# Attention scores of a chunk from three products on two halves of the array, instead of four products on the whole of it

## The chip, the core and the metric

The program runs on one core of a Trainium2 chip. The metric is the device time of one execution in microseconds (us), as the median over runs; the profile comes from one further execution.

## What is computed

Three stages follow one another: an attention with a threshold (4 batches, 8 heads, 576 positions, 64 values per head), a squared-ReLU feed-forward layer on its result (512 to 2048 to 512), and a mixture of 8 experts in which each token goes to one. The change touches only the scores of the attention:

```python
scores = scale * np.matmul(q, k.transpose(0, 1, 3, 2))
thresh = np.max(scores, axis=-1, keepdims=True) - tau
scores = np.where(scores >= thresh, scores, -1000000000.0)
attn = softmax(scores)          # written out in the reference
out = np.matmul(attn, v)
h = np.maximum(x @ w_in, 0.0); g = h * h; x = g @ w_out
# then: gate, one of 8 experts per token, two more products
```

## The kernel before

Products are taken in float32r, a rounded form of float32. To keep precision, an operand is split in a rounded part ("hi") and the rest ("lo", again rounded); a product of two operands is then a sum of terms hi·hi, hi·lo, lo·hi and, where wanted, lo·lo.

The attention runs over 16 pairs of heads (`pr`); a pair has 9 chunks of up to 128 queries (`STEPS`): four of head 0, four of head 1, and one (`hd == 2`) with the last 64 queries of both heads in one block-diagonal operand `xd`. That makes 144 chunks, numbered `n`. A chunk's work passes through all engines: scores on TensorE (`mm`, L636) against all 576 keys, in two halves of 288 in two banks of PSUM; maximum on VectorE (L639); exponential on ScalarE (L642); threshold and sum on VectorE (L651); division on GpSimd or ScalarE (L662, L695); five 128x128 transposes on TensorE (L705); copies out of PSUM on ScalarE (L713). Twice in a pair `t_av` (L733) multiplies with the values: ten products in two column halves of the array, 64 columns for each head, alternating between them. From the second batch on, the first feed-forward product (`t_h`, L843; 12 matmuls per unit, cut in three groups of four) of the batch before is interleaved with the chunks of the next batch.

The operands of a pair lie with head 0 on partitions 0-63 and head 1 on 64-127: `xk` and `xq` (index 0 hi, 1 lo). Three forms of the score product stand side by side in `t_chunk`:

- Chunks 0 to 3 (`n < EARLY`, L672) multiply directly on the head's 64 partitions, four terms for two halves: 8 matmuls of 64 rows. Chunks 0 and 1 are of head 0 (rows 0-63), chunks 2 and 3 of head 1 (rows 64-127).
- The block-diagonal chunk (`hd == 2`) uses 128 rows, three terms, 6 matmuls.
- All others (124 of the 144) use `opA` or `opB`, built for each head by `t_op`: for the keys, hi on partitions 0-63 and lo on 64-127; for the queries, the two parts in one order and in the other. Two passes of 128 rows, each for two halves, hold all four terms: 4 matmuls of 128 rows. To build them `t_op` issues five copies from SBUF to SBUF for each head on SyncE's queue (two `put_k`, one `put_q`, two `turn_q`), ten for a pair.

The order of all work is written out ahead by a list scheduler (`Graph.schedule`): each task has an engine, an assumed duration (`c_pe` and the like), a due time (`key`) and its reads and writes; engines then run their instructions in that fixed order. Buffers come from pools with a fixed number of slots; a buffer is given back after its last reader.

Of the kernel before, what the change touches and what calls it, by code (L numbers as in the profile page):

```python
# [9 lines left out]
F32 = mybir.dt.float32  # L10
# [201 lines left out]
def c_act(n, psum=False, ptr=0):  # L212
    return n / 1200 + (0.051 if psum else 0.093) + 0.093 * ptr


def c_dve(n, rate=1):
    return n / 960 / rate + 0.068


def c_pe(n):  # L220

    return n * 0.4227e-3 + 0.0123


def c_dma(nbytes):
    return 2.0 + nbytes / 150e3
# [35 lines left out]
def moa(ctx, tc, q, k, v, tau, w_in, w_out, wg, wog, w1, w2, ctab, coln, out):  # L262
    nc = tc.nc
    B, H, S, D = 4, 8, 576, 64
    P = 128
# [7 lines left out]
    HALF = S // 2  # L273
# [20 lines left out]
    OPN = S + 2 * 512  # L294
# [31 lines left out]
    g = Graph()  # L326
# [17 lines left out]
    def K(nm, pr):  # L344
        return PLACE[nm][pr >= NP]
# [88 lines left out]
        at = mk(nm, at, n, shape)  # L434
    at = 0
    for nm, n, shape in (
        ("xk", 2, [P, 2, S]), ("xq", 1, [P, 2, S]), ("xd", 1, [P, 2, P]),
        ("opA", 2, [P, OPN]), ("opB", 2, [P, OPN]),
    ):
        at = mk(nm, at, n, shape, F32R)  # L440
    ATT = 128 + 4 * NFC * P + 2 * 2 * NKC * 256 + 2 * (DFE // P) * 256
# [71 lines left out]
    def new(nm, tag):  # L513
        return Buf(ALL[nm], f"{nm}{tag}")

    def dma(fn, nbytes, r, w, key, q="SP", rel=0.0):
        dur = max(0.66, nbytes / 340e3)
        g.add(q, dur, fn, r, w, key, lat=c_dma(nbytes) - dur, rel=rel)

    raws, xks, xqs, xds, opb, xTb, wb = {}, {}, {}, {}, {}, {}, {}  # L520
# [27 lines left out]
    def q_tags(pr, x):  # L548
        return [(xqs[pr], x)] if pr else [(xqs[pr], x, i) for i in range(2)]
# [30 lines left out]
        g.add("ACT", c_act(S, False, nm == "q"), hi, [raw], [(xy, 0)], key - 1)  # L580
        g.add("DVE", 0.87, lo, [raw, (xy, 0)], [(xy, 1)], key - 1)

    def t_op(pr, j, key):

        xk, xq = xks[pr], xqs[pr]
        buf = opb[pr, j] = new("opB" if j else "opA", f"{pr}")
        rows = slice(64 * j, 64 * j + 64)
        q3 = lambda r: buf.t[r, S:].rearrange("p (x n) -> p x n", x=2).bitcast(F32)

        def put_k(x):  # L590
            nc.sync.dma_start(buf.t[64 * x : 64 * x + 64, :S].bitcast(F32), xk.t[rows, x].bitcast(F32))

        def put_q():
            nc.sync.dma_start(q3(slice(0, 64)), xq.t[rows, :, 64:].bitcast(F32))

        def turn_q(x):
            nc.sync.dma_start(q3(slice(64, 128))[:, 1 - x], xq.t[rows, x, 64:].bitcast(F32))

        parts = lambda xy, *xs: [t for x in xs for t in (q_tags(pr, x) if xy is xq else [(xy, x)])]
        for x in range(2):  # L600
            dma(lambda x=x: put_k(x), 64 * S * 4, parts(xk, x), [(buf, "k", x)], key)
        dma(put_q, 64 * 1024 * 4, parts(xq, 0, 1), [(buf, "q")], key)
        for x in range(2):
            dma(lambda x=x: turn_q(x), 64 * 512 * 4, parts(xq, x), [(buf, "t", x)], key)

    def t_diag(pr, key):

# [7 lines left out]
    def t_chunk(n, key):  # L615
        pr, st = divmod(n, NST)
        hd, c = STEPS[st]
        s = Buf(pS if n >= SWAP else pS0, f"s{n}")
        p = new("p", n)
        nm, th, sm = (new(x, n) for x in ("nm", "th", "sm"))  # L620
        heads = (0, 1) if hd == 2 else (hd,)
        halves = [slice(hf * HALF, (hf + 1) * HALF) for hf in range(2)]
        q0 = QOFF[c]
        xk = xks[pr]

        def mm():
            if hd == 2:

                xd = xds[pr].t
                ops = [(xd[:, x], xk.t[:, y]) for x, y in ((0, 0), (0, 1), (1, 0))]  # L630
            else:
                o = opb[pr, hd].t
                ops = [(o[:, S + i * 512 + q0 : S + i * 512 + q0 + P], o[:, :S]) for i in range(2)]
            for i, (qo, ko) in enumerate(ops):
                for hf in range(2):
                    nc.tensor.matmul(s.t[:, hf, :HALF], qo, ko[:, halves[hf]], start=(i == 0), stop=(i == len(ops) - 1))  # L636

        def mx():
            nc.vector.tensor_reduce(nm.t, s.t[:, :, :HALF], axis=AX.XY, op=ALU.max, negate=True)  # L639

        def ex():
            nc.scalar.activation(  # L642
                p.t[:, :S].rearrange("p (a n) -> p a n", a=2), s.t[:, :, :HALF], AF.Exp, bias=nm.t
            )

        def thr():
            nc.gpsimd.tensor_scalar(th.t, nm.t, -1.0, ntau, op0=ALU.mult, op1=ALU.add)  # L647

        def msk():
            p3 = p.t[:, :S].rearrange("p (a n) -> p a n", a=2)  # L650
            nc.vector.scalar_tensor_tensor(  # L651
                p3, s.t[:, :, :HALF], th.t, p3, op0=ALU.is_ge, op1=ALU.mult, accum_out=sm.t
            )

        def r1():
            nc.gpsimd.tensor_scalar(sm.t, sm.t, 1.0, 1e-9, op0=ALU.mult, op1=ALU.add)

        def r2():
            nc.vector.reciprocal(sm.t, sm.t)  # L659

        def nrm():
            nc.gpsimd.tensor_scalar(p.t[:, :S], p.t[:, :S], sm.t, 1.0, op0=ALU.mult, op1=ALU.mult)  # L662

        if n < EARLY:
            xq = xqs[pr]
            hr = slice(64 * hd, 64 * hd + 64)

            def mm():
                i = 0
                for qx, kx in ((0, 0), (0, 1), (1, 0), (1, 1)):  # L670
                    for hf in range(2):
                        nc.tensor.matmul(  # L672
                            s.t[:, hf, :HALF], xq.t[hr, qx, 64 + q0 : 64 + q0 + P], xk.t[hr, kx, halves[hf]],
                            start=(i == 0), stop=(i == 3),
                        )
                    i += 1

            rd = [(xk, x) for x in range(2)] + [(xq, x, 0) for x in range(2)]
            g.add("PE", c_pe(HALF) * 8, mm, rd, [s], key)
        elif hd == 2:  # L680
            rd = [(xk, x) for x in range(2)] + [(xds[pr], j) for j in range(2)]
            g.add("PE", c_pe(HALF) * 6, mm, rd, [s], key + K("scores", pr))
        else:
            o = opb[pr, hd]
            rd = [(o, "q")] + [(o, w, x) for w in "kt" for x in range(2)]
            g.add("PE", c_pe(HALF) * 4, mm, rd, [s], key + K("scores", pr))
        g.add("DVE", c_dve(S), mx, [s], [nm], key + K("max", pr))
        g.add("ACT", c_act(S, True, 1), ex, [s, nm], [p], key + K("exp", pr))
        g.add("POOL", 0.36, thr, [nm], [th], key + K("bound", pr))
        g.add("DVE", c_dve(S) + 0.085, msk, [s, th], [p, sm], key + K("mask", pr))  # L690
        g.add("POOL", 0.22, r1, [], [sm], key + K("sum", pr))
        g.add("DVE", 0.09, r2, [], [sm], key + K("sum", pr))
        if pr < NP and hd == 0 and c % 2:
            g.add("ACT", c_act(S, False, 1),
                  lambda: nc.scalar.activation(p.t[:, :S], p.t[:, :S], AF.Copy, scale=sm.t), [sm], [p],  # L695
                  key + K("norm", pr))
        else:
            g.add("POOL", 0.85, nrm, [sm], [p], key + K("norm", pr))

        for x, (a, z) in enumerate(TCUT):  # L700
            ps = Buf(pT[x], f"pT{n}_{x}")

            def tr(ps=ps, a=a, z=z):
                for i in range(a, z):
                    nc.tensor.transpose(ps.t[:, i - a], p.t[:, i * P : (i + 1) * P], ident)  # L705

            g.add("PE", 0.109 * (z - a), tr, [p], [ps], key + K("turn", pr))
            for j, gi, c0, w, off in PARTS[st]:
                if (pr, gi) not in ptb:
                    ptb[pr, gi] = new("pt", f"{pr}_{gi}")  # L710
                pt = ptb[pr, gi]
                g.add("ACT", c_act((z - a) * w, True),
                      lambda pt=pt, ps=ps, j=j, a=a, z=z, c0=c0, w=w, off=off: nc.scalar.activation(  # L713
                          pt.t[:, j, a:z, off : off + w], ps.t[:, :, c0 : c0 + w], AF.Copy),
                      [ps], [(pt, j, off, x)], key + K("parts", pr))
# [240 lines left out]
    rows = {}  # L956
# [412 lines left out]
    def pair_prep(pr, key):  # L1369
        for nm in "kqv":  # L1370
            t_load(pr, nm, key - 8)
        for nm in "kq":
            t_qk(pr, nm, key)
        for j in range(2):
            t_op(pr, j, key)
        t_diag(pr, key)

    pair_prep(0, -100)
    t_fill(5)
    wkey = {i: (W0 + 2.25 * i) * T0 for i in range(NFC)}  # L1380

    for pr in range(NPR):
# [3 lines left out]
        for st in range(NST):  # L1386
            n = pr * NST + st
# [54 lines left out]
    for i in range(22):  # L1442
        n = 160 if i < 8 else 256
# [12 lines left out]
    with tc.If(more > 0):  # L1456
        for tab, lo, hi, U in ((tab2, S2, NL2, 2), (tab1, S1, NL1, 1)):
            n = nc.values_load(tabn[0:1, 2 - U : 3 - U], min_val=0, max_val=hi)
# [49 lines left out]
```

## Time and profile before

| | us |
|---|---|
| time, median of 3 runs | 967.85 |
| lowest and highest of them | 965.61 and 968.86 |
| the profiled execution's own time | 965.47 |
| its span in the trace | 963.7 |
| TensorE busy in it | 932.3 (97%) |
| VectorE / ScalarE / GpSimd busy | 716.4 / 645.6 / 361.3 |

TensorE is busy nearly throughout. The trace models the ends of matmuls, and they overlap in the engine's pipeline: a row's duration is not what a matmul costs in a row of others. What it costs is the distance from one start to the next. A row of the timeline merges neighbouring instructions of one line; with n of them, the distance is the row's length less the duration of the last one, divided by n - 1. A window of 10 ns shows the instructions in flight at that moment, and the start of the oldest.

### The profile page before, as it was taken

Reading aid. Unit: us, or ns where it says so; the run is one execution under the profiler, and the core shown is the slowest. Engines: PE = TensorE matmul, PEld = TensorE weight load, DVE = VectorE, ACT = ScalarE, POOL = GpSimd, SP = SyncE. Lnnn points to the kernel's source line nnn. Section 1 sums busy time; section 2 is a strip of 40 time slices with the busy share of each in tenths; the row PEclk is TensorE's granted clock in tenths of the full one; section 3 lists DMA queues with packets and bytes.
Section 4 is the critical chain, followed back from the end, with each engine's and each line's share of the span. In section 5 each row is a group of like instructions: output and inputs, shape, how many; then the busy total and the mean of one; then the engine's idle time right before and its main releaser. Section 6 shows DMA issues by size and latency. Waiting matters only on the chain. (4 is left out here: it accounts for less than half of the span.)

```text
span 963.7 us, 20604 instructions
## 1 busy us (share of the span) xinstructions
PE 932.3 (97%) x6842; PEld 846.0 (88%) x6842; DVE 716.4 (74%) x1635; ACT 645.6 (67%) x1431; POOL 361.3 (37%) x607
## 2 busy tenths in 40 slices
PE   7899999999999999999999999999898999999996
PEld 6667889889889889989999999999887989889895
DVE  6898988877777777788558767898778677777720
ACT  5898888878678777787554444444648676876731
POOL 4556778875656766642101000010113111211300
PEclk9999999999999999999999999999999999999999
DMA  6785797767778766478455888566959867977700
GB/s 176 181 221 141 204 253 201 213 166 212 234 214 231 228 198 201 158 226 246 136 143 133 190 185 194 134 171 140 260 170 338 307 229 262 309 248 257 264 23 25
DMA packets 162565, 193.25 MB, mean 201 GB/s; under 512 B 23567, under 2 KB 113167, under 8 KB 162450
## 3 DMA queue, kind: packets, MB, share of 16 engines
q1 hardware_dynamic: 158210, 181.33, 65.2%
q0 software_dynamic: 4096, 10.52, 3.5%
q8 instruction: 56, 0.92, 0.4%
q14 instruction: 59, 0.48, 0.2%
q10 hardware_dynamic: 144, 0.00, 0.0%
HBM read 122.39 MB, written 43.20 MB: 172 GB/s over the span
## 5 line engine op out<-in xcount | busy, mean ns | idle before, releaser
L651 DVE SCALAR_TENSOR_TENSOR memf<-banks,memf 128x576 f32<-128x576 f32 x144 | 116.3, 814 | 43.4 <-ACT memf L642 27.0
L843 PE MATMUL banks<-memr,w 128*128 128x288 f32 x960 | 145.0, 299 | 1.3 <-DVE memr L740 1.3
L843 PEld LDWEIGHTS banks<-memr,w 128*128 128x128 f32 x960 | 130.9, 188 | 5.3 <-issue 3.8
L1004 PE MATMUL banks<-w,memr 128*128 128x256 f32 x864 | 126.9, 284 | 0.0
L713 ACT ACTIVATE pt<-banks 128x384 f32<-128x384 f32 (+2 forms) x320 | 114.2, 419 | 14.0 <-PE banks L705 13.5
L642 ACT ACTIVATE memf<-banks,memf 128x576 f32<-128x576 f32 x144 | 107.1, 753 | 20.1 <-DVE memf L639 13.6
L984 ACT ACTIVATE memr<-memf 128x512 fp32r<-128x512 f32 x126 | 77.7, 631 | 63.3 <-PE banks L1004 57.4
L639 DVE TENSOR_REDUCE memf<-banks 128x1 f32<-128x576 f32 x144 | 107.5, 750 | 16.3 <-PE banks L636 14.6
L662 POOL TENSOR_SCALAR memf<-memf 128x576 f32<-128x576 f32 x136 | 112.9, 832 | 13.0 <-DVE memf L659 7.0
L636 PE MATMUL banks<-memr 128*128 128x288 f32 x592 | 108.8, 308 | 5.3 <-DVE memf L651 3.4
L1004 PEld LDWEIGHTS banks<-w,memr 128*128 128x128 f32 x864 | 112.3, 190 | 0.3
L705 PE MATMUL banks<-ident,memf 128*128 128x128 f32 x720 | 104.6, 274 | 6.3 <-ACT pt L713 4.2
L1004 PE MATMUL banks<-memr 128*128 128x256 f32 x648 | 99.6, 285 | 0.0
L705 PEld LDWEIGHTS banks<-ident,memf 128*128 128x128 f32 x720 | 84.2, 140 | 14.6 <-POOL memf L647 4.7
L880 POOL TENSOR_TENSOR memf<-memf 128x288 f32<-128x288 f32 x88 | 71.5, 822 | 66.4 <-DVE memf L880 37.0
L636 PEld LDWEIGHTS banks<-memr 128*128 128x128 f32 x592 | 83.8, 188 | 13.8 <-DVE memf L651 7.1
L1301 PE MATMUL banks<-memr,w 128*128 128x256 f32 x504 | 91.4, 283 | 0.9 <-DVE memr L1311 0.9
L1140 POOL DMA_INDIRECT lst<-memf x18 | 18.7, 1039 | 193.6 <-DVE memf L1132 108.8
L988 DVE TENSOR_TENSOR memr<-memf,memr 128x512 fp32r<-128x512 f32 x126 | 82.9, 695 | 10.5 <-ACT memr L984 10.5
L843 PE MATMUL banks<-memr 128*128 128x288 f32 x576 | 87.9, 299 | 0.9 <-ACT memf L849 0.9
L1004 PEld LDWEIGHTS banks<-memr 128*128 128x128 f32 x648 | 87.1, 190 | 0.0
L733 PE MATMUL banks<-pt,memf 128*64 128x256 f32 (+1 forms) x640 | 85.0, 411 | 1.2 <-DVE memf L651 0.9
(153 smaller groups left out, 1778.4 us busy)
## 6 DMA issues: line engine op xcount, KB each, us to landing
memf<-in_moe_w_dram SPq DMA_DIRECT2D x104, 512.0 KB
r_scr<-memf SPq DMA_DIRECT2D x192, 144.0 KB
memf<-r_scr SPq DMA_DIRECT2D x51, 512.0 KB
memr<-memr SPq DMA_DIRECT2D x64, 144.0 KB
memr<-memr SPq DMA_DIRECT2D x64, 128.0 KB
memr<-memr SPq DMA_DIRECT2D x32, 256.0 KB
memf<-in_moe_w_in_dram SPq DMA_DIRECT2D x32, 256.0 KB
memf<-in_moe_w_out_dram SPq DMA_DIRECT2D x32, 256.0 KB
```

The source lines that it names most:

```text
L636: nc.tensor.matmul(s.t[:, hf, :HALF], qo, ko[:, halves[hf]], start=(i == 0), stop=(i == len(ops) - 1))
L639: nc.vector.tensor_reduce(nm.t, s.t[:, :, :HALF], axis=AX.XY, op=ALU.max, negate=True)
L642: nc.scalar.activation(p.t[:, :S].rearrange("p (a n) -> p a n", a=2), s.t[:, :, :HALF], AF.Exp, bias=nm.t)
L651: nc.vector.scalar_tensor_tensor(p3, s.t[:, :, :HALF], th.t, p3, op0=ALU.is_ge, op1=ALU.mult, accum_out=sm.t)
L662: nc.gpsimd.tensor_scalar(p.t[:, :S], p.t[:, :S], sm.t, 1.0, op0=ALU.mult, op1=ALU.mult)
L705: nc.tensor.transpose(ps.t[:, i - a], p.t[:, i * P : (i + 1) * P], ident)
L713: lambda pt=pt, ps=ps, j=j, a=a, z=z, c0=c0, w=w, off=off: nc.scalar.activation(pt.t[:, j, a:z, off : off + w], ps.t[:, :, c0 : c0 + w], A ...
L733: nc.tensor.matmul(out(slice(64 * j, 64 * j + 64)), raw.t[:, j, c], pt.t[:, j, c, :N], start=(c == 0), stop=(c == NQ - 1))
L843: nc.tensor.matmul(ps.t[:, :HALF], wv[:, a, kc], xT.t[:, x, kc, half], start=(i == 0), stop=(i == len(seq) - 1),)
L988: lambda d=d, sq=sq: nc.vector.tensor_tensor(d(1), sq(), d(0).bitcast(F32), op=ALU.subtract),
L1004: nc.tensor.matmul(ps.t[:, :QT], o.t[:, a, f], w.t[:, x, cc], start=(f == 0 and i == 0), stop=(f == 7 and i == 2))
L1301: nc.tensor.matmul(ps.t[:, :256], w1b[kc][fc // 4].t[:, a, (fc % 4) * P : (fc % 4 + 1) * P], x2.t[:, x, kc], start=(i == 0), stop=(i == 11))
```

## The change

Three of the four terms are kept (hi·hi, hi·lo, lo·hi). For the 124 chunks of one head, the first half of the keys is multiplied on array rows 0-63 and the second half on rows 64-127: 6 matmuls of 64 rows in the order first half, second half, first half, and so on. Half `hd` of the keys is read where `xk` and `xq` hold that head; for the other half, `t_op` copies that half's keys and all queries of the chunked part to the opposite partitions, in one buffer `ox` per pair: two copies of keys and two of queries for a pair. The four early chunks stay on their head's rows and do 6 matmuls instead of 8. `xq` has two slots instead of one, since the chunks now read it; `xk` and `xq` are read until the pair's last chunk.

```diff
-        ("xk", 2, [P, 2, S]), ("xq", 1, [P, 2, S]), ("xd", 1, [P, 2, P]),
-        ("opA", 2, [P, OPN]), ("opB", 2, [P, OPN]),
+        ("xk", 2, [P, 2, S]), ("xq", 2, [P, 2, S]), ("xd", 1, [P, 2, P]),
+        ("ox", 2, [P, OPN]),
...
+    ROWS = [slice(0, 64), slice(64, 128)]
+    HALVES = [slice(hf * HALF, (hf + 1) * HALF) for hf in range(2)]
+
+    def t_op(pr, key):
...
+        def put_k(j):
+            nc.sync.dma_start(
+                buf.t[ROWS[1 - j], :S].rearrange("p (x n) -> p x n", x=2).bitcast(F32),
+                xk.t[ROWS[j], :, HALVES[1 - j]].bitcast(F32))
+
+        def put_q(j):
+            nc.sync.dma_start(
+                buf.t[ROWS[1 - j], S:].rearrange("p (x n) -> p x n", x=2).bitcast(F32),
+                xq.t[ROWS[j], :, 64:].bitcast(F32))
+
+        for j in range(2):
+            dma(lambda j=j: put_k(j), 64 * S * 4, [(xk, x) for x in range(2)], [(buf, "k", j)], key)
+            dma(lambda j=j: put_q(j), 64 * 1024 * 4, q_tags(pr, 0) + q_tags(pr, 1), [(buf, "q", j)], key)
...
         def mm():
...
+            for i, (x, y) in enumerate(((0, 0), (0, 1), (1, 0))):
                 for hf in range(2):
-                    nc.tensor.matmul(s.t[:, hf, :HALF], qo, ko[:, halves[hf]], start=(i == 0), stop=(i == len(ops) - 1))
+                    r = ROWS[hf]
+                    if hd == 2:
+                        qo, ko = xds[pr].t[:, x], xk.t[:, y, halves[hf]]
+                    elif hf == hd:
+                        qo, ko = xq.t[r, x, 64 + q0 : 64 + q0 + P], xk.t[r, y, halves[hf]]
+                    else:
+                        o = opb[pr].t
+                        qo, ko = o[r, S + x * 512 + q0 : S + x * 512 + q0 + P], o[r, y * HALF : (y + 1) * HALF]
+                    nc.tensor.matmul(s.t[:, hf, :HALF], qo, ko, start=(i == 0), stop=(i == 2))
...
-                for qx, kx in ((0, 0), (0, 1), (1, 0), (1, 1)):
+                for i, (qx, kx) in enumerate(((0, 0), (0, 1), (1, 0))):
...
-            g.add("PE", c_pe(HALF) * 8, mm, rd, [s], key)
+            g.add("PE", c_pe(HALF) * 6, mm, rd, [s], key)
...
-            g.add("PE", c_pe(HALF) * 4, mm, rd, [s], key + K("scores", pr))
+            rd = [(opb[pr], "k", hd), (opb[pr], "q", hd)] + [(xk, x) for x in range(2)] + q_tags(pr, 0) + q_tags(pr, 1)
+            g.add("PE", c_pe(HALF) * 3 + 0.02, mm, rd, [s], key + K("scores", pr))
```

## Rows read from the trace of the kernel before

**Rows 1.** Busy time by stretch: engines with instruction counts, granted clock, DMA share, GB/s

```profile
0.00:12.00 12.00, 9.80 (x54) 9.01 (x54) 5.93 (x14) 4.03 (x5) 3.85 (x22) 1.00 0.67 182
12.00:95.00 83.00, 72.37 (x528) 54.78 (x528) 73.17 (x182) 70.51 (x160) 47.66 (x110) 1.00 0.70 180
95.00:430.00 335.00, 331.94 (x2555) 296.67 (x2553) 264.56 (x596) 266.79 (x653) 232.37 (x402) 1.00 0.72 209
490.00:950.00 460.00, 453.78 (x3242) 422.70 (x3242) 333.54 (x769) 263.65 (x523) 66.04 (x60) 1.00 0.70 205
```

**Rows 2.** Waits of TensorE, 95 to 430 us: all of them

```profile
PE banks L636 <- DVE memf L651: 1.3, 3, 0.8
PE banks L843 <- ACT memf L849: 0.9, 1, 0.9
PE banks L705 <- POOL memf L656: 0.7, 1, 0.7
```

**Rows 3.** Score matmuls by line: first 95 to 430 us, then 12 to 95 us

```profile
L636 PE MATMUL banks<-memr 128*128 128x288 f32 x434 | 78.9, 306 | 1.4 <-DVE memf L651 1.3
...
L636 PE MATMUL banks<-memr 128*128 128x288 f32 x160 | 30.3, 315 | 3.9 <-DVE memf L651 2.1 <-DMA memr<-memr 1.5
```

**Rows 4.** TensorE's timeline from 219.2 us: start, length, merged instructions

```profile
219.31 1.76 PE L843 MATMUL banks<-memr 128*128 128x288 f32 x12
220.91 0.71 PE L705 MATMUL banks<-ident,memf 128*128 128x128 f32 x5
221.37 0.77 PE L636 MATMUL banks<-memr 128*128 128x288 f32 x4
221.98 1.74 PE L843 MATMUL banks<-memr 128*128 128x288 f32 x12
```

**Rows 5.** Early chunks on 64 rows: timeline, then durations (minimum, median, maximum)

```profile
6.25 3.59 PE L672 MATMUL banks<-memr 64*128 64x288 f32 x24
10.77 1.32 PE L672 MATMUL banks<-memr 64*128 64x288 f32 x8 [0.93 <-DVE memf L651]
...
10.77 0.40 PE L672 MATMUL banks<-memr 64*128 64x288 f32 x1 [0.93 <-DVE memf L651]
...
L672 PE MATMUL banks<-memr x32: 288/292/606, 6.3 to 11.8; 64*128 64x288 f32 x32
```

**Rows 6.** L672 in two 10 ns windows: TensorE matmuls, then weight loads in flight

```profile
8.66:8.67 0.01, 0.01 (x4) 0.01 (x4) 1.00 0.00 0
9.22:9.23 0.01, 0.01 (x2) 0.01 (x1) 1.00 0.95 205
```

**Rows 7.** In flight on TensorE at 182.50, 184.80 and 185.18 us, around a values product

```profile
182.25 0.29 PE L843 MATMUL banks<-memr,w 128*128 128x288 f32 x1
182.47 0.44 PE L733 MATMUL banks<-pt,memf 128*64 128x256 f32 x2
...
184.46 0.39 PE L733 MATMUL banks<-pt,memf 128*64 128x256 f32 x2
184.78 0.40 PE L636 MATMUL banks<-memr 128*128 128x288 f32 x1
...
185.01 0.43 PE L636 MATMUL banks<-memr 128*128 128x288 f32 x2
```

**Rows 8.** Timeline: a values product, and transposes that follow one

```profile
99.81 2.38 PE L733 MATMUL banks<-pt,memf 128*64 128x256 f32 x20
...
215.51 0.76 PE L705 MATMUL banks<-ident,memf 128*128 128x128 f32 x5
```

**Rows 9.** In flight on TensorE around two 32-row transposes (511.99, 512.18, 512.56 us)

```profile
511.73 0.28 PE L1004 MATMUL banks<-w,memr 128*128 128x256 f32 x1
511.94 0.24 PE L1078 MATMUL banks<-ident,memf 32*128 32x32 f32 x1
...
512.17 0.39 PE L1004 MATMUL banks<-w,memr 128*128 128x256 f32 x1
...
512.40 0.40 PE L1004 MATMUL banks<-w,memr 128*128 128x256 f32 x2
```

**Rows 10.** Timeline around matmuls with 32 active columns

```profile
510.10 0.28 PE L1004 MATMUL banks<-memr 128*128 128x256 f32 x1
510.21 0.28 PE L1069 MATMUL banks<-memr 128*32 128x256 f32 x1
...
510.21 1.08 PE L1069 MATMUL banks<-memr 128*32 128x256 f32 x8
511.13 0.40 PE L1004 MATMUL banks<-memr 128*128 128x256 f32 x2
```

**Rows 11.** SyncE's queue: copies for the operands of one pair, and the next load

```profile
39.37 0.59 SPq L591 DMA_DIRECT2D memr<-memr  x1
40.00 0.62 SPq L594 DMA_DIRECT2D memr<-memr  x1
40.66 0.61 SPq L597 DMA_DIRECT2D memr<-memr  x1
41.37 1.48 SPq L612 DMA_DIRECT2D memr<-memr  x2
42.90 0.58 SPq L533 DMA_DIRECT2D memf<-in_k_dram  x1
```

More of the change, by code (lines that the diff above doesn't have):

```diff
@@ L581, in t_qk @@
         g.add("DVE", 0.87, lo, [raw, (xy, 0)], [(xy, 1)], key - 1)
-    def t_op(pr, j, key):
+    ROWS = [slice(0, 64), slice(64, 128)]
+    HALVES = [slice(hf * HALF, (hf + 1) * HALF) for hf in range(2)]
+    def t_op(pr, key):
         xk, xq = xks[pr], xqs[pr]
[L586 to L604, printed above, removed]
+        buf = opb[pr] = new("ox", f"{pr}")
+        def put_k(j):
[9 more added lines that the diff above has]
+            dma(lambda j=j: put_q(j), 64 * 1024 * 4, q_tags(pr, 0) + q_tags(pr, 1), [(buf, "q", j)], key)
     def t_diag(pr, key):
@@ L621, in t_chunk @@
         heads = (0, 1) if hd == 2 else (hd,)
-        halves = [slice(hf * HALF, (hf + 1) * HALF) for hf in range(2)]
+        halves = HALVES
         q0 = QOFF[c]
-        xk = xks[pr]
+        xk, xq = xks[pr], xqs[pr]
         def mm():
[L627 to L634, printed above, removed]
-                for hf in range(2):
-                    nc.tensor.matmul(s.t[:, hf, :HALF], qo, ko[:, halves[hf]], start=(i == 0), stop=(i == len(ops) - 1))
+            for i, (x, y) in enumerate(((0, 0), (0, 1), (1, 0))):
+                for hf in range(2):
+                    r = ROWS[hf]
[7 more added lines that the diff above has]
+                    nc.tensor.matmul(s.t[:, hf, :HALF], qo, ko, start=(i == 0), stop=(i == 2))
         def mx():
@@ L664, in t_chunk @@
         if n < EARLY:
-            xq = xqs[pr]
-            hr = slice(64 * hd, 64 * hd + 64)
+            hr = ROWS[hd]
             def mm():
-                i = 0
-                for qx, kx in ((0, 0), (0, 1), (1, 0), (1, 1)):
+                for i, (qx, kx) in enumerate(((0, 0), (0, 1), (1, 0))):
                     for hf in range(2):
@@ L673, in mm @@
                             s.t[:, hf, :HALF], xq.t[hr, qx, 64 + q0 : 64 + q0 + P], xk.t[hr, kx, halves[hf]],
-                            start=(i == 0), stop=(i == 3),
+                            start=(i == 0), stop=(i == 2),
                         )
-                    i += 1
             rd = [(xk, x) for x in range(2)] + [(xq, x, 0) for x in range(2)]
-            g.add("PE", c_pe(HALF) * 8, mm, rd, [s], key)
+            g.add("PE", c_pe(HALF) * 6, mm, rd, [s], key)
         elif hd == 2:
@@ L683, in t_chunk @@
         else:
-            o = opb[pr, hd]
-            rd = [(o, "q")] + [(o, w, x) for w in "kt" for x in range(2)]
-            g.add("PE", c_pe(HALF) * 4, mm, rd, [s], key + K("scores", pr))
+            rd = [(opb[pr], "k", hd), (opb[pr], "q", hd)] + [(xk, x) for x in range(2)] + q_tags(pr, 0) + q_tags(pr, 1)
+            g.add("PE", c_pe(HALF) * 3 + 0.02, mm, rd, [s], key + K("scores", pr))
         g.add("DVE", c_dve(S), mx, [s], [nm], key + K("max", pr))
@@ L1373, in pair_prep @@
             t_qk(pr, nm, key)
-        for j in range(2):
-            t_op(pr, j, key)
+        t_op(pr, key)
         t_diag(pr, key)
```

## The prediction

> **What bounds the kernel now.** I read the busy time by stretch first. From 95 to 430 us, where chunks and first feed-forward products share TensorE, it is busy 331.9 of 335 us and its clock is granted in full; the other engines have a fifth or more of their time free [rows 1]. The waits of TensorE in that stretch add up to 2.9 us, none of them for a DMA [rows 2]. So there the time is the sum of TensorE's instructions, and a change is priced by start-to-start distances. From 12 to 95 us it is otherwise: TensorE has 10.6 us idle of 83, VectorE is busy 73.2 and ScalarE 70.5 [rows 1]; a part of TensorE's extra work can vanish there. After 430 us no scores are computed; that part only shifts.
>
> The timeline shows the grain. Twelve feed-forward matmuls of 288 columns last 1.76 us with the last one's 0.29 us, (1.76 - 0.29) / 11 = 0.13 us each; a chunk's four score matmuls lie between transposes and feed-forward groups, mostly alone [rows 4]. Matmuls of only 64 rows keep the same distance: eight last 1.32 us, the first one's row is 0.40 us, (1.32 - 0.40) / 7 = 0.131 us [rows 5]. A pass of 288 columns costs 0.131 us whether it uses 64 rows or 128.
>
> **How many chunks are concerned.** Matmuls of L636 from 95 us on are 434, of which two began before the edge; 432 = 90 chunks of 4 and 12 block-diagonal ones of 6 [rows 3]. Before it are 160: 34 chunks of 4 and 4 of 6 (160 = 136 + 24) [rows 3]. I went through TensorE's timeline group by group (a stretch of it is [rows 4]). The 90 chunks form 89 groups: 81 come after transposes or feed-forward matmuls, 8 after a values product; 32 are followed by transposes, 51 by feed-forward matmuls, 6 by a values product. The 34 early ones form 31 groups, nearly all between transposes.
>
> **What is removed.** If the two halves of the array run side by side, a chunk needs three pass times instead of four: 0.131 less some ns for the second stream's start, 0.126 us. Do they? The four early chunks show it. Chunks 0 and 1 are on rows 0-63, 2 and 3 on 64-127, with no wait between 1 and 2. At 8.66 us, where chunk 1 ends and chunk 2 begins, four matmuls and four weight loads are in flight; at 9.22 us, when chunk 2 runs alone, two and one [rows 6]. So two streams on different row halves run at once, loads included. That is a block of one half beside a block of the other; the change alternates them one by one. The values product alternates like that on column halves, and its matmuls come in pairs [rows 7]. Over 90 chunks this saves 90 x 0.126 = 11.3 us.
>
> **What is added: the switches.** The trace has no chunk in which TensorE goes straight from 128 rows to 64 or back: the early chunks are bordered by waits. The nearest rows are two other narrow forms.
> - Into the values product (64 columns): it starts 0.22 us after the feed-forward matmul before it, against 0.13 in a row: 0.09 us [rows 7].
> - Out of it: ten pairs last 2.38 us with the last one's 0.38, so 0.22 a pair [rows 8]; the score matmul behind starts 0.32 us after the last pair: 0.10 us more. That matmul's own successor comes 0.23 us later instead of 0.13, because its weight load lay open: 0.10 us [rows 7]. Transposes behind it last 0.76 instead of 0.71 us: 0.05 us [rows 8, 4].
> - Two transposes on 32 rows: 0.21 us after the matmul before, where 0.12 is usual: 0.09 us. After them the wide matmuls again lose 0.23 - 0.12 = 0.11 us on the first load, behind no wait [rows 9]. So narrow rows are charged like narrow columns.
> - Against it: matmuls with 32 active columns at the array's first columns cost nothing, 0.11 us in, and (0.40 - 0.28) = 0.12 from the first wide one to the next [rows 10]. A narrow shape alone is not the cause; addressing the array in parts is.
> - The exposed first load of 64 rows: 0.40 - 0.29 = 0.11 us [rows 5]; both halves' first loads can share it [rows 6].
>
> So a 64-row group costs between nothing [rows 10] and the full switch [rows 7, 9]. I take the full one, since the 32-row form is nearest and its cost stood there without a wait behind it. Entry is 0.09 + 0.11 = 0.20 us, exit 0.10 + 0.10 = 0.20 before feed-forward matmuls and 0.10 + 0.05 = 0.15 before transposes. Beside a values product the switch is paid today, so it adds nothing: entries 81 x 0.20 = 16.2; exits 51 x 0.20 + 32 x 0.15 = 15.0. Less 11.3, that is +19.9 us on the path.
>
> The Trainium skill speaks against this change in the same sense: TensorEngine Tiling (Array Packing), Tiling Modes, states that changing the tiling mode, and not merely the tile, drains TensorE. No row here shows it for 64 rows; by that rule the switches above hold, without it their 31.2 us fall away.
>
> **The first stretch.** 31 groups x 0.35 less 34 x 0.126 = 10.9 - 4.3 = 6.6 us more on TensorE, against 10.6 us idle. Of it between 6.6 and nothing shows; the one wait of scores for a DMA, 1.5 us [rows 3], may go with the shorter copies, so the low end is -1.5. I take a third, +2.2, as TensorE's idle time there exceeds it. The early chunks lose 8 matmuls, 8 x 0.131 = 1.05 us; most of that is beside other work, I take -0.3 (0 to -1.05).
>
> **Copies and buffers: nothing.** Ten copies for a pair become four, each about 0.6 us of SyncE's queue [rows 11]: 6 x 16 x 0.6 = 58 us less on a queue that TensorE never waits for after 95 us [rows 2]. The key copies now wait for both parts of `xk`; behind them on that queue stand the query copies, the two of `xd` and the next pair's load [rows 11], which move earlier all the same. `xk` and `xq` are held to the ninth chunk; nine chunks take some 30 us (335 us for the 102 chunks of that stretch, 3.3 us each), and a second slot covers the next pair. Without that cover the pair's load, split and copies, some 7 us of SyncE's issues alone (10 x 0.6 and 1.48) [rows 11], would stand in the open once a pair. Maximum, exponential and mask are unchanged and have slack.
>
> **Sum.** 19.9 + 2.2 - 0.3 = +21.8 us on the profiled execution's 965.47, 987.3 us. That execution is 2.4 us under the median of the runs, 967.85; at the median's level I forecast 989.5 us. The scheduler is told 0.42 us for the new chunk and knows no switch, so it may order the work differently; I allow 4 us either way.
>
> **The rivals.**
> - *No switch between 64 and 128 rows.* Place: every entry and exit from 95 to 430 us. Only the saved pass remains, -11.3, with -0.3 and about -0.5 from the rest: 955.8 us, faster. For it: [rows 6], [rows 10]. Against it: [rows 9]. The point from which it decides: 164 entries and exits that are not shared must cost less than 11.3 / 164 = 0.07 us each. The Trainium skill would have it so in TensorE: Matmul & The Clock Gate, Part 3, where packed tiles cost one matmul and about 4 ns for each further tile, with no word of neighbours; [rows 6] agree on the overlap and say nothing of the borders.
> - *Half a switch.* Only the drain is paid and the loads stay hidden, or the reverse: 81 x 0.09 + 83 x 0.10 - 11.3 = +4.3, with the first stretch 972 us (968 to 979).
> - *Alternating halves don't overlap*, so the change doesn't do what it says: 6 passes instead of 3, +0.393 us for each of 90 chunks, 35 us more, and some 12 in the first stretch, whose idle time is then used up: 1035 us. [rows 6, 7] speak against it.
>
> **Chances.** Forecast 0.72 (own range 980 to 1000, from the first stretch's ends and the order), no switch 0.13, half a switch 0.09, no overlap 0.06. The range 968 to 1000 holds the first and the third, 0.81. Under 0.3%, about 2.9 us, this kernel cannot be told from no change; faster 0.13, same 0.04, slower 0.83.
>
> **What would show it.** In the changed kernel's timeline a group of six score matmuls of 64 rows should start 0.22 us after the feed-forward matmul before it and last about 0.67 us (0.11 + 2 x 0.131 + some ns + 0.29), and the next group should start about 0.3 us after its last pair, with its second matmul 0.23 us on. TensorE should stay without waits from 95 us, and that stretch should end some 20 us later. A group that starts 0.13 us after its predecessor means no switch, starts 0.131 us apart inside a group mean no overlap. Scores that wait for copies or for `xk` would make the buffer step wrong.

## The result, and the profile after

The changed kernel takes 978.86 us (977.96 to 982.04), the kernel before 968.36 us beside it: a ratio of 1.0122, 95% interval 1.0097 to 1.0146, +9 to +14 us. (The ratios here and below are estimated over all runs and are not the quotients of the two medians, here 1.0108.) Measured again, in the second set of experiments (`after_same_chip`) and beside more runs of the kernel before, it is 978.31 against 964.9 us, ratio 1.0143, interval 1.0125 to 1.0161, +12 to +16 us. The change makes the kernel slower, by 10.5 and 13.4 us between the medians: half to six tenths of the forecast's +21.8.

Busy time by stretch in the changed kernel, with the columns of [rows 1], and below it its score matmuls on 64 rows, which stand where [rows 3] stood:

```profile
12.00:95.00 83.00, 75.34 (x577) 51.21 (x577) 72.55 (x178) 69.89 (x155) 47.76 (x108) 0.95 0.48 126
95.00:430.00 335.00, 333.96 (x2636) 275.67 (x2636) 254.08 (x573) 255.80 (x621) 225.22 (x394) 1.00 0.57 171
...
L636 PE MATMUL banks<-memr 64*128 64x288 f32 x546 | 59.6, 325 | 0.6 <-DVE memf L651 0.6
```

TensorE's idle time from 95 to 430 us has shrunk from 3.1 us to 1.0 us (335 - 333.96). 546 matmuls of 64 rows are 91 chunks of six. Its waits in that stretch are now 1.1 us instead of 2.9 [rows 2].

TensorE's timeline, for comparison with [rows 4]: a chunk's scores stand alone between feed-forward matmuls (L839) and transposes (L701).

```profile
221.19 1.83 PE L839 MATMUL banks<-memr 128*128 128x288 f32 x12
222.95 0.67 PE L636 MATMUL banks<-memr 64*128 64x288 f32 x6
223.54 0.77 PE L701 MATMUL banks<-ident,memf 128*128 128x128 f32 x5
224.24 0.67 PE L636 MATMUL banks<-memr 64*128 64x288 f32 x6
```

What is in flight at 222.97, 223.56, 224.85 and 225.25 us shows the borders of those two groups:

```profile
222.72 0.29 PE L839 MATMUL banks<-memr 128*128 128x288 f32 x1
222.95 0.40 PE L636 MATMUL banks<-memr 64*128 64x288 f32 x2
...
223.32 0.30 PE L636 MATMUL banks<-memr 64*128 64x288 f32 x2
223.54 0.33 PE L701 MATMUL banks<-ident,memf 128*128 128x128 f32 x1
...
224.61 0.30 PE L636 MATMUL banks<-memr 64*128 64x288 f32 x2
224.84 0.40 PE L839 MATMUL banks<-memr 128*128 128x288 f32 x1
...
225.07 0.43 PE L839 MATMUL banks<-memr 128*128 128x288 f32 x2
```

The first score matmul starts 222.95 - 222.72 = 0.23 us after its predecessor, where 0.13 is usual, and its row is 0.40 long instead of 0.29: drain 0.09 to 0.10, open weight load 0.11. Two matmuls start together. Behind the group the next kind starts 0.22 to 0.23 us after the last pair, and the second feed-forward matmul another 0.23 us later: again a drain and an open load. Each price of the forecast stands in these rows. (The forecast's sign said about 0.3 us behind the last pair: it had carried over the distance of the values product's pairs, 0.22 us. The price above the usual distance, 0.22 - 0.13, is the one that it took.)

Where the time went is seen from when the first and the last feed-forward matmul start; between them lies the shared stretch, in which TensorE has hardly any time free: its rows leave 4.3 us idle in the kernel before, 1.5 and 1.0 us in the changed kernel's two profiles. First the kernel before (its first and last are 92.3 and 485.5), then the changed kernel (93.9 and 500.4): durations, then first and last start.

```profile
L843 PE MATMUL banks<-memr,w x960: 288/295/406, 139.2 to 485.5; 128*128 128x288 f32 x192
L843 PE MATMUL banks<-memr x576: 288/295/403, 92.3 to 453.7; 128*128 128x288 f32 x192
...
L839 PE MATMUL banks<-memr,w x960: 288/295/404, 140.4 to 500.4; 128*128 128x288 f32 x192
L839 PE MATMUL banks<-memr x576: 288/295/406, 93.9 to 468.6; 128*128 128x288 f32 x192
```

So the first stretch grew by 1.6 us and the shared stretch from 393.2 to 406.5, +13.3 us. The rest of the program, which the change does not touch, lasted 478.2 us before (963.7 - 485.5) and 479.7 after (980.1 - 500.4); over all kernels below it lies between 474.9 and 480.8 us without order, so differences of 2 or 3 us between whole profiles mean nothing. The shared stretch repeats better: 406.5 and 405.6 us in the two profiles of the changed kernel, 393.2 in the kernel before and 393.5 in e11, whose edit touches the first four chunks alone.

The kernels of the next section in the same numbers (their own profiles; "us" is the median of the runs, "over before" the ratio with its interval):

| kernel | us | over before | first feed-forward | last | shared stretch |
|---|---|---|---|---|---|
| before | 964.4 to 968.4 | | 92.3 | 485.5 | 393.2 |
| changed (first profile) | 978.86 | 1.0122 (1.0097 to 1.0146) | 93.9 | 500.4 | 406.5 |
| after_same_chip | 978.31 | 1.0143 (1.0125 to 1.0161) | 94.4 | 500.0 | 405.6 |
| e1_first_pass_64 | 995.57 | 1.0301 (1.0257 to 1.0346) | 97.7 | 518.6 | 420.9 |
| e2_own_rows | 1023.58 | 1.0591 (1.0537 to 1.0644) | 106.6 | 548.4 | 441.8 |
| e3_two_chunks | 978.68 | 1.0142 (1.0095 to 1.0190) | 102.5 | 499.6 | 397.1 |
| e7_two_late | 978.75 | 1.0154 (1.0130 to 1.0178) | 92.1 | 500.1 | 408.0 |
| e4_early_four | 982.76 | 1.0172 (1.0130 to 1.0215) | 96.5 | 502.9 | 406.4 |
| e11_before_early | 965.29 | 1.0003 (0.9983 to 1.0022) | 95.2 | 488.6 | 393.5 |
| e6_told_switch | 982.41 | 1.0187 (1.0168 to 1.0205) | 93.1 | 502.2 | 409.1 |
| e8_copies_twice | 987.07 | 1.0227 (1.0206 to 1.0248) | 102.5 | 511.0 | 408.5 |
| e10_copies_late | 981.07 | 1.0172 (1.0144 to 1.0201) | 95.3 | 501.9 | 406.6 |
| e9_two_more | 988.31 | 1.0255 (1.0225 to 1.0284) | 94.9 | 507.2 | 412.4 |
| e12_half_by_half | 977.86 | 1.0136 (1.0106 to 1.0166) | 94.6 | 501.4 | 406.8 |

### The profile page after: what moved, and what is told of

The parts are those of the page before. It is cut to its first block, busy times and chain, and to the rows that moved or that the text cites. A ratio compares the mean times of both kernels' runs of the same rounds, so it can differ in the third digit from the quotient of the medians.

```text
span 980.1 us, 20904 instructions
## 1 busy us (share of the span) xinstructions
PE 953.7 (97%) x7082; PEld 835.2 (85%) x7082; DVE 718.4 (73%) x1635; ACT 646.0 (66%) x1431; POOL 362.4 (37%) x607
## 5 line engine op out<-in xcount | busy, mean ns | idle before, releaser
L839 PE MATMUL banks<-memr,w 128*128 128x288 f32 x960 | 150.1, 303 | 0.5 <-DVE memr L736 0.5
L839 PEld LDWEIGHTS banks<-memr,w 128*128 128x128 f32 x960 | 130.5, 188 | 9.2 <-issue 7.9
L1000 PE MATMUL banks<-w,memr 128*128 128x256 f32 x864 | 124.4, 283 | 0.0
L701 PE MATMUL banks<-ident,memf 128*128 128x128 f32 x720 | 110.4, 281 | 4.7 <-ACT pt L709 2.7
L636 PE MATMUL banks<-memr 64*128 64x288 f32 (+1 forms) x840 | 100.1, 326 | 2.2 <-DVE memf L651 2.1
L876 POOL TENSOR_TENSOR memf<-memf 128x288 f32<-128x288 f32 x88 | 76.1, 871 | 66.8 <-DVE memf L876 42.7
L701 PEld LDWEIGHTS banks<-ident,memf 128*128 128x128 f32 x720 | 82.4, 142 | 19.8 <-issue 7.6
L636 PEld LDWEIGHTS banks<-memr 64*128 64x128 f32 (+1 forms) x840 | 68.6, 188 | 27.5 <-issue 15.3
L839 PE MATMUL banks<-memr 128*128 128x288 f32 x576 | 90.5, 303 | 0.0
L1278 DVE TENSOR_TENSOR w<-memf,w 128x512 fp32r<-128x512 f32 x113 | 75.6, 688 | 16.8 <-ACT w L1275 14.2
```

Of the source, the lines that this page charges most:

```text
L636: nc.tensor.matmul(s.t[:, hf, :HALF], qo, ko, start=(i == 0), stop=(i == 2))
L839: nc.tensor.matmul(ps.t[:, :HALF], wv[:, a, kc], xT.t[:, x, kc, half], start=(i == 0), stop=(i == len(seq) - 1),)
L1000: nc.tensor.matmul(ps.t[:, :QT], o.t[:, a, f], w.t[:, x, cc], start=(f == 0 and i == 0), stop=(f == 7 and i == 2))
```

## The experiments

**The switch alone.** The kernel before with its first pass on 64 rows: no pass saved, nothing side by side, only borders added.

```diff
+                rw = (slice(0, 64), slice(0, P))
-                ops = [(o[:, S + i * 512 + q0 : ... + P], o[:, :S]) for i in range(2)]
+                ops = [(o[rw[i], S + i * 512 + q0 : ... + P], o[rw[i], :S]) for i in range(2)]
```

> The kernel before, with its first pass cut to rows 0-63 (it leaves out the lo-lo term, as the changed kernel does); the second pass stays on 128 rows. No pass is saved and no halves run side by side: a chunk only gains two switches, into 64 rows and back to 128. Switch theory (0.20 us in, 0.20 us out before a 128-row matmul, 8 entries shared with the values product): 90 x 0.40 - 8 x 0.20 = +34 us from 95 us on, and 34 x 0.40 = 13.6 us in the first stretch, of which some 3 to 8 show: about 1007 us. Rival (a border between 64 and 128 rows is free, the changed kernel is slower for another reason): within 3 us of the kernel before, 968 us. Rival (only the drain or only the load is charged): about 985 to 990 us.

In flight at 113.87 and 114.34 us in that kernel (L844 is its feed-forward line, L637 its scores):

```profile
113.63 0.29 PE L844 MATMUL banks<-memr 128*128 128x288 f32 x1
113.86 0.40 PE L637 MATMUL banks<-memr 64*128 64x288 f32 x1
...
114.09 0.62 PE L637 MATMUL banks<-memr 64*128 64x288 f32 x2
```

Entry 0.23 us and an open load (0.40 instead of 0.29); inside the chunk, where the second row merges the last matmul of 64 rows and the first of 128, the latter's row is 0.40 long again, so it starts 0.62 - 0.40 = 0.22 us after it, where 0.13 is usual. Borders between 64 and 128 rows are paid in both directions, by drain and by load. The kernel is 31.2 us over the kernel before by the medians (25 to 33 by the interval); the shared stretch grew by 27.8 us. A free border (0 us) is ruled out. By the total alone the result lies between the full and the half switch; the rows decide for the full one. At the trace's prices (82 entries at 0.199, 91 inner borders at 0.195 us) it should have been 34.0 us: 6.2 us did not show, while the idle time in the shared stretch fell by 3.0 us, from 4.3 to 1.3.

**The overlap alone.** Both halves on the rows of the chunk's own head; the copies go on, unread.

```diff
-                    elif hf == hd:
-                        qo, ko = xq.t[r, x, ...], xk.t[r, y, halves[hf]]
-                    else:
-                        o = opb[pr].t
-                        qo, ko = o[r, ...], o[r, y * HALF : (y + 1) * HALF]
+                    else:
+                        r = ROWS[hd]
+                        qo, ko = xq.t[r, x, 64 + q0 : 64 + q0 + P], xk.t[r, y, halves[hf]]
...
-            g.add("PE", c_pe(HALF) * 3 + 0.02, mm, rd, [s], ...)
+            g.add("PE", c_pe(HALF) * 6, mm, rd, [s], ...)
```

> The changed kernel, but both halves of the keys are multiplied on the rows of the chunk's own head, all six matmuls on the same 64 rows; the copies to the other rows are still issued, nobody reads them. Theory (halves on different rows run fully side by side): six passes instead of three, +0.386 us for each of 91 chunks = +35 us, and 3 to 10 us of the 13 in the first stretch, so about 1017 to 1024 us. Rival (halves overlap only in part, say half): about 1000 us. Rival (no overlap): as the changed kernel, 979 us.

A chunk's group in its timeline:

```profile
224.75 1.06 PE L634 MATMUL banks<-memr 64*128 64x288 f32 x6
```

1.06 us against 0.67 with the halves side by side: 0.39 us, three passes. The total is as forecast by full overlap, and the shared stretch is 35.3 us longer than in the changed kernel, for 91 x 0.386 = 35.1 us of added work. In a stretch that is already full, all of an addition shows.

**How much free time the kernel before had.** A known price without a switch: the first pass issued twice.

```diff
+            if hd < 2:
+                for hf in range(2):
+                    nc.tensor.matmul(s.t[:, hf, :HALF], ops[0][0], ops[0][1][:, halves[hf]], start=True, stop=True)
             for i, (qo, ko) in enumerate(ops):
```

> The kernel before with the first pass of each of the 124 chunks issued twice (the second time it starts the sum anew, so the result is the same): two matmuls of 128 rows more per chunk, no switch, a known price of 2 x 0.131 us. From the first feed-forward matmul to the last, 90 chunks x 0.262 = 23.6 us more work. If TensorE had no time free there, 393.2 us become 416.8. Theory for the forecast's excess: some 4 to 6 us of short waits lie between TensorE's groups and longer groups cover them; then 411 to 413 us. In all, 15 to 24 us over the kernel before, by what the first stretch shows of its 8.9 us.

Its stretch from 95 to 430 us, and the first and last feed-forward matmul:

```profile
95.00:430.00 335.00, 334.40 (x2591) 303.21 (x2590) 248.47 (x566) 252.79 (x611) 221.25 (x390) 1.00 0.68 197
...
L846 PE MATMUL banks<-memr,w x960: 288/295/406, 143.4 to 507.2; 128*128 128x288 f32 x192
L846 PE MATMUL banks<-memr x576: 288/295/401, 94.9 to 475.4; 128*128 128x288 f32 x192
```

The shared stretch is 412.4 us, 19.2 more, for 23.3 us of additional distance between the chunk's matmuls. 4.1 us vanish, and TensorE's idle time from 95 to 430 us falls from 3.1 to 0.6 us. TensorE's groups follow one another in the same order in both kernels, so the place can be read off: in 52 places a chunk's scores come behind a feed-forward matmul, and their first matmul starts 0.175 us after it on average before, 0.133 us here. That is 2.2 of the 4.1 us; another 0.8 lie between scores and transposes. Not all of it is listed as idle, since a start that comes up to 0.16 us late is still covered by the row of the matmul before (0.29 us long, 0.13 us apart). The amount is the theory's: the kernel before held some 4 us of short waits between TensorE's groups, and added work got those free of charge.

**Fewer switches: two chunks in one group.** The scores of neighbouring chunks of one head as one task of 12 matmuls; first for all chunks, then from the fifth pair on.

```diff
+        if n >= EARLY and st in (0, 2, 4, 7):      # e7: n >= SWAP
+            s2 = held[n + 1] = Buf(pS if n >= SWAP else pS0, f"s{n + 1}")
...
+                def both():
+                    mm()
+                    mm(s2, ahead[n])
+                g.add("PE", 2 * (c_pe(HALF) * 3 + 0.02), both, rd, [s, s2], ...)
```

> The changed kernel, but the scores of two neighbouring chunks of one head are one task of TensorE, 12 matmuls in a row, both score buffers held together. Half of the groups of 64 rows fall away, each worth 0.35 to 0.40 us. Switch theory: 91 chunks in some 46 groups instead of 87, 40 x 0.38 = 15 us less after 95 us, so 964 us, if the other engines keep up with chunks that come in twos. Rival (two score buffers freed together stall TensorE): the switches fall but waits of scores for VectorE take their place, 979 us or more. Rival (switches are not the cause): 979 us without new waits.

> As e3_two_chunks, the scores of two neighbouring chunks as one group of 12 matmuls, but only from the fifth pair of heads on (chunk 36), so that the first batch keeps the changed kernel's order. e3 gained in the later stretch (397.1 us from the first feed-forward matmul to the last, 406.5 in the changed kernel, 393.2 before) and lost in the first (the first feed-forward matmul at 102.5 us instead of 93.9). Switch theory: it keeps the gain and not the loss, 9 us under the changed kernel. Rival (what e3 gained in the later stretch was only work that its slow start had moved forward or back): as the changed kernel.

The groups of 64 rows between 95 and 430 us fell from 87 to 47 in both, counted on the timeline, and neither kernel is faster than the changed one. The stretch from 95 to 430 us, first of e3, then of e7:

```profile
95.00:430.00 335.00, 330.59 (x2711) 280.07 (x2711) 262.50 (x587) 257.70 (x634) 228.79 (x401) 0.99 0.59 175
...
95.00:430.00 335.00, 325.72 (x2637) 276.26 (x2637) 254.14 (x581) 253.08 (x623) 227.06 (x398) 0.98 0.59 172
```

TensorE's idle time rises from 1.0 us to 4.4 and 9.3. In e7 nearly all of it is listed as waits of transposes (L717) for ScalarE's copies out of PSUM (L725) and for GpSimd's division (L671), and of feed-forward and values products; scores (L645) wait 0.8 us for VectorE:

```profile
PE banks L717 <- ACT pt L725: 3.2, 3, 1.6
PE banks L717 <- POOL memf L671: 3.1, 3, 2.2
...
PE banks L645 <- DVE memf L660: 0.8, 1, 0.8
```

The trace shows one such gap and what follows it:

```profile
224.16 1.07 PE L645 MATMUL banks<-memr 64*128 64x288 f32 x12
...
233.46 0.82 PE L717 MATMUL banks<-ident,memf 128*128 128x128 f32 x5 [2.16 <-POOL memf L671]
234.21 2.21 PE L645 MATMUL banks<-memr 64*128 64x288 f32 x12
```

0.6 us after a gap of 2.16 us without work TensorE's granted clock falls to half, 1.2 instead of 2.4 GHz, and a group of 12 takes 2.21 us instead of 1.07. The clock is at half for 6.8 and 3.4 us in e7's shared stretch; half of that, some 5 us, is lost. So of the 15 us that 40 switches fewer are worth by their price, waits (8.3 us more than in the changed kernel) and the clock take back 13; with the shared stretch 1.5 to 2.4 us longer than the changed kernel's, some 3 us stay unexplained. The rival with the two score buffers has the time right but not the waits: its scores that wait for VectorE are 0.8 us, and the engines behind the scores make up the rest. That chunks in twos cause these waits is inferred from the two kernels, not shown apart from their order. e3 looks better in the shared stretch and loses the same in the first one, 8.6 us; how much of that is work done earlier and how much is its smaller idle time stays open. No version here beats the kernel before.

**The early chunks and the clock.**

```diff
-                for i, (qx, kx) in enumerate(((0, 0), (0, 1), (1, 0))):
+                for i, (qx, kx) in enumerate(((0, 0), (0, 1), (1, 0), (1, 1))):
...
-            g.add("PE", c_pe(HALF) * 6, mm, rd, [s], key)
+            g.add("PE", c_pe(HALF) * 8, mm, rd, [s], key)
```

> The changed kernel with the four early chunks at four terms (8 matmuls) again. In the changed kernel's profile the granted clock is at half from 9.4 to 19.5 us, after TensorE had been idle 0.35 us at 7 us and 1.4 us from 9.2 us; the kernel before shows no such stretch. If the eight matmuls fewer bring that on, the clock stays full here and the first stretch is 1 to 3 us shorter: 976 to 978 us. If the clock falls for another reason: 979 us, with the half-clock stretch still there.

The granted clock stays full over the first 95 us, as foretold, yet the first feed-forward matmul comes 2.6 us later than in the changed kernel, not sooner, and 982.76 us lies outside both expectations. Nor do the missing matmuls bring the half clock on: e1 does all eight and is at half clock from 8.9 to 22.5 us, e10 does six and keeps the clock full up to its first feed-forward matmul. What brings it on stays open. No cost of it shows: e4 and e10, at full clock, reach the first feed-forward matmul at 96.5 and 95.3 us, the changed kernel, at half clock for 10.2 us, at 93.9 and 94.4. TensorE is idle there for 7.7 of 83 us (12 to 95 us), so it is not alone the bound; but the orders differ, and a run that changes the clock alone was not made. The opposite edit, three terms in the kernel before and nothing else of the change:

> The kernel before with one part of the change alone: the four early chunks at three terms, 6 matmuls instead of 8, on the same 64 rows; all else as before. The changed kernel with four terms there (e4) was 4 us slower than the changed kernel. If the three terms alone bring that, this is 1 to 4 us faster than the kernel before; if e4's loss came from the order that the scheduler chose, within 1.5 us of the kernel before.

No difference can be measured. e4's median lies 4.4 us above the changed kernel's, but the intervals of the two ratios overlap and its shared stretch is the changed kernel's (406.4 us); if there is a loss, it is put down to the order rather than to the four terms, which is inferred, not shown.

**The scheduler told of the switch.**

```diff
-            g.add("PE", c_pe(HALF) * 3 + 0.02, mm, rd, [s], ...)
+            g.add("PE", c_pe(HALF) * 3 + 0.40, mm, rd, [s], ...)
```

> The changed kernel with the assumed duration of its score task raised by 0.38 us in the scheduler, to what its group really takes with both switches; no instruction differs but the order. If the wrong assumption costs time (work planned for moments when TensorE is still busy), this is 2 to 6 us faster than the changed kernel. If TensorE is simply full, as the switch theory has it, order changes nothing: within 3 us of it.

4 us slower than the changed kernel on the same chip, against both expectations: the shared stretch is 409.1 instead of 405.6 us. Its order has 173 borders that are not shared with a values product, where the changed kernel has 157: 16 more, at 0.14 to 0.20 us each, make some 3 of these 3.5 us. An order's worth here lies largely in how many borders it leaves, and a truer duration did not find a better one.

**The copies.** Each a second time, into a buffer that nobody reads; then the same from the fifth pair of heads on.

```diff
+        bufs = [opb[pr], new("oy", f"{pr}")]       # e10: only if pr >= NP
-        for j in range(2):
-            dma(lambda j=j: put_k(j), ...)
+        for j, buf in ((j, buf) for j in range(2) for buf in bufs):
+            dma(lambda j=j, buf=buf: put_k(j, buf), ...)
...
```

> The changed kernel with each copy of keys and queries issued a second time into a buffer that nobody reads: eight copies and 1600 KB for a pair, the bytes of the kernel before. Theory (the copies are beside the path): within 2 us of the changed kernel. Rival (the lighter copies are why the change cost less than forecast): 4 to 8 us slower than the changed kernel.

> As e8_copies_twice, each copy issued a second time into a buffer that nobody reads, but only from the fifth pair of heads on. e8 was 8.8 us slower than the changed kernel; its first feed-forward matmul came 8.1 us later, the stretch after it took 2.9 us more. Theory: copies cost only in the first stretch, where a pair's operands are waited for; then this is within 2 us of the changed kernel, 978 us. Rival (SyncE's queue or the traffic slows the later stretch too): 3 us or more slower, 981 us or above.

e8 is 8.8 us slower than the changed kernel by the medians, 11.8 us in the two profiles: 8.1 of these lie before the first feed-forward matmul, 2.9 in the shared stretch and 0.7 behind it. In the timeline the first values product stands at 26.21 us, behind a wait and at half clock; in the changed kernel (second row, of after_same_chip) it started at 23.65 us and took 2.38 us:

```profile
26.21 4.53 PE L730 MATMUL banks<-pt,memf 128*64 128x256 f32 x20 [2.02 <-DVE memf L652]
...
23.65 2.38 PE L729 MATMUL banks<-pt,memf 128*64 128x256 f32 x20 [0.41 <-DVE memf L651]
```

e10, without the early copies, has the changed kernel's first stretch (95.3 us) and 406.6 us in the shared one (405.6 and 406.5 in the changed kernel's two profiles). Its median, 981.07 us, is 2.8 us higher and so meets the rival's line of 981 us; but the intervals of the two ratios overlap, and of the 4.3 us between its profile and after_same_chip's 2.4 lie behind the shared stretch, where no copy runs and the clock is at half for 6.8 us from 707 us on. So the copies cost nothing visible in the shared stretch, and up to some 3 us in the time stay open. The doubled list of the first pairs does go with a loss, but by which way is not shown: from 12 to 95 us TensorE waits for a copy once, 0.6 us, while the early half clock lasts 20.5 us instead of 10.2 and the order differs.

**Order inside a group.** Three matmuls on rows 0-63, then three on 64-127, instead of alternating.

```diff
+            if hd < 2:
+                order.sort(key=lambda o: o[3])     # by half
...
```

> The changed kernel with the six matmuls of a chunk ordered by half, three on rows 0-63 and then three on rows 64-127, instead of alternating; same matmuls, same switches. If the engine lets the second row half start beside the first whatever the order, within 2 us of the changed kernel. If it starts instructions in the written order and a weight load waits for the one before it on the same rows, the second half starts late: up to 2 x 0.131 us for each of 91 chunks, 10 to 24 us slower.

As fast as the changed kernel. In flight at 223.66 us:

```profile
223.40 0.29 PE L843 MATMUL banks<-memr 128*128 128x288 f32 x1
223.62 0.41 PE L640 MATMUL banks<-memr 64*128 64x288 f32 x2
```

Two matmuls of the group have begun within 0.01 us (the median over the groups from 95 us on is 0.01 us too), though the first of the other half is written three places later. The trace does not name a matmul's rows; but on the same rows they start 0.13 us apart (e2), so these two are of different halves. The overlap does not need the alternating order.

**The changed kernel once more,** beside e6, e7 and e8.

> The changed kernel itself, beside the next three on one chip. By the first comparison 1.0 to 1.5% over the kernel before. The switch theory, with its counts from the profile of the changed kernel (78 entries at 0.20, 45 exits at 0.19 before feed-forward matmuls, 32 at 0.14 before transposes, less 91 x 0.124 for the saved pass), gives +17.6 us from the first feed-forward matmul to the last; the profile had +13.3 there. The theory of the remaining 4 us: short waits of TensorE in the kernel before that the longer groups cover. Here the profile should again have +12 to +15 us in that stretch against 393.2 us before.

+13.4 us by the medians, 405.6 us in the shared stretch, +12.4.

## Why the prediction was right, and where it was too high

The sign, the mechanism and every price of a border held; the forecast of +21.8 us was too high for +10.5 (first set) to +13.4 us (second). The measured 978.86 and 978.31 us lie below the forecast's own range, 980 to 1000; they fall into the stated one, 968 to 1000, only because it was drawn to hold the half switch too. By the time alone that rival (972 us, 968 to 979) fits better: the rows at the borders decide for the full switch, not the total. (A slip in the sum: 967.85 + 21.8 is 989.65 us, not 989.5.)

- *What bounds the kernel.* Right: TensorE, from 95 us on. The term that was too large is the +19.9 us on the path; it measured 12.4 to 13.3, and the step behind it stands in the same paragraph of the prediction. It read 331.9 busy us of 335 and 2.9 us of waits [rows 1, 2] and then put all of the sum on the path. The gaps are real free time: after the change 1.0 us of them is left, and e9, in the old order, measures what they swallow, 4.1 us of 23.3. The other additions agree: 34.0 us priced against 27.8 in e1; 18.0 against 12.4 to 13.3 in the changed kernel; and 35.1 against 35.3 in e2, counted from the changed kernel, where hardly anything was left to swallow. In the changed kernel the listed idle time of the shared stretch fell by 2.8 to 3.4 us of the 5 that are missing; that the rest went the same way is inferred from e9, as the order of its groups is another. So the stretch ended 14.5 to 14.9 us later, not some 20.
- *The saved pass.* Right. Pairs start within 0.01 us of each other, and e2 prices the overlap at 0.39 us for a chunk.
- *The switches.* Right in kind and size, in both directions, with drain and load (the rows of the changed kernel, e1). The Trainium skill, TensorEngine Tiling (Array Packing), Tiling Modes, has the drain at every change of mode; these runs agree and put 0.09 us to it, and they show beside it an open weight load of 0.11 us, or 0.05 before transposes. The number of borders was taken from the old order, 164 that are not shared; the new order has 157 (78 entries, 79 exits), because more groups lie beside a values product and four chunks stand next to another. By the same prices that makes 78 x 0.20 + 45 x 0.194 + 32 x 0.143 - 91 x 0.124 = 17.6 us instead of 19.9; two exits into the block-diagonal chunk are left out of it and, at e1's 0.195 us, make it 18.0 us.
- *The first stretch.* +1.6 and +2.1 us against +2.2 taken: right, though by a mixture of things that was not foreseen. The granted clock is at half for 10.2 us there, at no cost that a run shows.
- *Copies at no cost.* No loss in the shared stretch is visible (e10), though its time leaves up to some 3 us open. In the first pairs doubling them goes with a loss of 8 us (e8). The shorter list of copies may so have been worth something there; a run that takes it apart from the order was not made.
- *The order.* The 4 us allowed are what e6 lost.
- *The rivals.* No switch: e1 excludes it, and its break-even point, 0.07 us for a border, is passed by a factor of two and more. Half a switch: the rows show both halves. No overlap: e2.

## What to carry to other kernels

Before filling idle rows of a matmul, look at how its neighbours are addressed: here a pass saved 0.124 us and two borders cost 0.34 to 0.40 us, so by these prices (an estimate; no run saved more than one) a group must save three to four passes of 288 columns before it pays, unless it stands beside another that is addressed in the same parts. Where an engine is nearly full, subtract the idle time that the profile still lists from a sum before it goes on the path: 4.3 us were listed here, and 4 to 6 us of each addition vanished. Groups of twice the size to save borders brought waits of their own, mostly of transposes for the engines before and behind them.

## What the runs showed of the hardware that was not expected

- Matmuls on different row halves started side by side in either written order (e12: 0.01 us apart, with two matmuls of the first half written between). The Trainium skill, TensorE: Matmul & The Clock Gate, Part 3, says that matmuls start and end strictly in program order; the measurement differs, if the program ran in the order in which the kernel writes it, which the trace does not show.
- Weight loads of the same 64 rows run beside that half's matmuls: in e2 six of them on the same rows take 1.06 us, 0.11 + 5 x 0.13 + 0.29, as for 128 rows. The Trainium skill, in the same Part 3, has loads overlap with matmuls in flight only where the row groups differ; its paragraph on the mechanism also lets a load go ahead into a background weight buffer, and these rows agree with that.
- A gap of 2.16 us in TensorE's work was followed by a half clock (e7), and 12 score matmuls then took 2.21 us instead of 1.07. So long a gap is not needed: in e1 the clock fell at 8.9 us, when TensorE had been idle for only 0.15 and 0.35 us since 1.3 us.
